# Four heads per pass on 128 partitions: block transposes on VectorE, block-diagonal fp32 bounds, score operands built by DMA, and an FFN in chunks of 512 tokens

## The chip, the cores and the metric

The kernel runs on one core of one Trainium2 chip. The metric is the device time of one execution in microseconds. A core has these engines: TensorE (PE in the profile; its weight loads are the row PEld), VectorE (DVE), ScalarE (ACT), GpSimd (POOL) and SyncE (SP, which here only issues DMA).

## The reference

An attention that looks only at the best chunks of keys, followed by a gated feed-forward network (FFN). Batch 4, 8 heads, 768 positions, 64 dimensions a head; the FFN sees 3072 tokens of 512 and has 1536 hidden channels.

```python
k_min, k_max = min and max of k over chunks of 32 positions      # 24 chunks
ub = sum_d max(q*k_min, q*k_max)                                 # upper bound per query and chunk
top = the 6 best chunks by ub among the causal ones              # per query
scores = (q @ k.T) / 8, masked to the chosen chunks and to the past
attn = softmax(scores) @ v                                       # heads side by side -> x, 512 wide
xn = x / sqrt(mean(x*x) + 1e-6) * rms_g
out = (silu(xn @ w_gate) * (xn @ w_val)) @ w_out
```

## The kernel before

It takes two heads at a time (16 pairs). It loads q and k with positions on partitions, transposes them on TensorE in fp32 and spreads the result on ScalarE and VectorE. The bounds use sum(relu(q)\*k_max - relu(-q)\*k_min): both parts stand on 128 partitions, so that one fp32 matmul gives 128 queries' bounds for up to 24 chunks. A query's threshold is its sixth best bound. The choice is written as 24 more rows under q, against rows of 30000 under k, so that the score matmul itself drops chunks. The causal triangle is added by one more matmul.

```python
# prep of a pair, per group of 128-position blocks
nc.tensor.transpose(pq[...], qnat[...], ident_f[:])                     # L158, fp32, likewise pk L177
nc.scalar.activation(out=QM[0][0:D, cols], in_=pq[0:D, :], func=ACT.Relu)
# ... three more relus, copies to QS and KE on ScalarE and VectorE, min and max of pk over chunks
# selection, per 128 queries and head (12 units a pair)
nc.tensor.matmul(ubp[:, 0:n_i], QM[hl][:, i*P:(i+1)*P], KM[hl][:, 0:n_i], ...)   # L213, fp32
# VectorE adds the causal mask and takes the best eight, GpSimd compares with the threshold (L253)
nc.tensor.transpose(stp[0:n_i, :], selq[:, 0:n_i], ident_b[:])          # L224
nc.vector.tensor_copy(QS[hl][D:D+n_i, i*P:(i+1)*P], stp[0:n_i, :])
# scoring, per head, 256 queries and group kg of 256 keys
nc.tensor.matmul(sc[:, e, :], keh[:, kb*P:(kb+1)*P], qsh[:, qcols], ...)          # L279
nc.tensor.matmul(sc[:, e, e*P:(e+1)*P], ident_b[:], trimask[:], ...)    # L284, the last group only
nc.scalar.activation(out=pt[:], in_=sc[:], func=ACT.Exp, scale=SCALE)   # 128x512
nc.tensor.matmul(avn[:], pt[:, e, s*P:(s+1)*P], vext[:, kb, hl, :], ...)          # L303
emit_ffn_slice(1)                                     # one piece of the FFN, if there is one
# ... [cut] after a batch's four pairs: x statistics, transposes of x, and its FFN pieces are queued,
# in a chunk of 512 and one of 256 tokens: 12+4 and 12+2 pieces
```

The softmax here doesn't subtract the row's maximum and nothing guards it: scores larger than these inputs give would overflow.

Of the kernel before, what the change touches and what calls it, by code (L numbers as in the profile page):

```python
# [8 lines left out]
FP32 = mybir.dt.float32  # L9
# [5 lines left out]
BIGE = 30000.0  # L15
BIGT = -30000.0
BIGC = 1.0e30
THRFLOOR = -5.0e29
# [3 lines left out]
def kernel(  # L22
# [14 lines left out]
    assert (P, D) == (128, 64) and S % 256 == 0  # L37
    CH = 32
    NCH = S // CH
    NT = S // P  # L40
    NQT = S // 256
    NP = H // 2
    DM = H * D
    DFF = moe_w_gate.shape[1]
    NHT = DFF // P
    NTOK = B * S
    NTT = NTOK // P
# [4 lines left out]
    prep = ctx.enter_context(tc.tile_pool(name="prep", bufs=3))  # L52
    headp = ctx.enter_context(tc.tile_pool(name="headp", bufs=6))
    sel = ctx.enter_context(tc.tile_pool(name="sel", bufs=8))
    work = ctx.enter_context(tc.tile_pool(name="work", bufs=6))
    evict = ctx.enter_context(tc.tile_pool(name="evict", bufs=6))
    hhp = ctx.enter_context(tc.tile_pool(name="hhp", bufs=NHT + 4))
    ffn = ctx.enter_context(tc.tile_pool(name="ffn", bufs=3))
    psA = ctx.enter_context(tc.tile_pool(name="psA", bufs=6, space=bass.MemoryType.PSUM))
    psF = ctx.enter_context(tc.tile_pool(name="psF", bufs=2, space=bass.MemoryType.PSUM))  # L60

    ident_f = const.tile([P, P], FP32, name="ident_f")
    masks.make_identity(nc, ident_f[:])
    ident_b = const.tile([P, P], BF16, name="ident_b")
    nc.vector.tensor_copy(ident_b[:], ident_f[:])

    trimask = const.tile([P, P], BF16, name="trimask")
    nc.gpsimd.memset(trimask[:], 0.0)
    nc.gpsimd.affine_select(
        out=trimask[:], in_=trimask[:], compare_op=ALU.is_ge, fill=BIGT,  # L70
        base=0, pattern=[[1, P]], channel_multiplier=-1,
    )

    cmf = const.tile([P, NT, NCH], FP32, name="cmf")
    nc.gpsimd.memset(cmf[:], 0.0)
    for g4 in range(4):
        nc.gpsimd.affine_select(
            out=cmf[32 * g4:32 * (g4 + 1), :, :],
            in_=cmf[32 * g4:32 * (g4 + 1), :, :],
            compare_op=ALU.is_ge, fill=-BIGC,  # L80
            base=g4, pattern=[[4, NT], [-1, NCH]], channel_multiplier=0,
        )

    e_all = const.tile([NCH, S], BF16, name="e_all")
    nc.gpsimd.memset(e_all[:], BIGE)
    nc.gpsimd.affine_select(
        out=e_all[:], in_=e_all[:], compare_op=ALU.is_ge, fill=0.0,
        base=0, pattern=[[1, S]], channel_multiplier=-CH,
    )
    nc.gpsimd.affine_select(  # L90
        out=e_all[:], in_=e_all[:], compare_op=ALU.is_ge, fill=0.0,
        base=CH - 1, pattern=[[-1, S]], channel_multiplier=CH,
    )

    eps6 = const.tile([P, 1], FP32, name="eps6")
    nc.gpsimd.memset(eps6[:], 1.0e-6)
    thrfloor = const.tile([P, 1], FP32, name="thrfloor")
    nc.gpsimd.memset(thrfloor[:], THRFLOOR)

    rmsg = const.tile([P, NP], FP32, name="rmsg")  # L100
    nc.sync.dma_start(out=rmsg[:], in_=moe_rms_g.rearrange("(g p) -> p g", p=P))

    ss_all = const.tile([P, NTT], FP32, name="ss_all")
    ri_all = const.tile([P, NTT], FP32, name="ri_all")

    xnat = [persist.tile([P, DM], BF16, name=f"xnat{tt}") for tt in range(NTT)]
    xsT = persist.tile([P, NP, NTOK], BF16, name="xsT")

    sel_count = [0]
    ffn_queue: list = []  # L110

    def emit_ffn_slice(n=1):
        for _ in range(n):
            if ffn_queue:
                ffn_queue.pop(0)()

    def emit_prep(b, pr):
        h0 = 2 * pr
        qnat = prep.tile([P, NT, 2, D], FP32, name="qnat")
        knat = prep.tile([P, NT, 2, D], FP32, name="knat")  # L120
        vext = prep.tile([P, NT, 2, D + 1], BF16, name="vext")
        for hh in range(2):
            nc.sync.dma_start(
                out=qnat[:, :, hh, :],
                in_=q[b, h0 + hh, :, :].rearrange("(blk pp) d -> pp blk d", pp=P),
            )
        for hh in range(2):
            nc.scalar.dma_start(
                out=knat[:, :, hh, :],
                in_=k[b, h0 + hh, :, :].rearrange("(blk pp) d -> pp blk d", pp=P),  # L130
            )
        nc.gpsimd.memset(vext[:, :, :, D:D + 1], 1.0)
        for hh in range(2):
            nc.gpsimd.dma_start(
                out=vext[:, :, hh, 0:D],
                in_=v[b, h0 + hh, :, :].rearrange("(blk pp) d -> pp blk d", pp=P),
            )

        kmx = prep.tile([P, NCH], FP32, name="kmx")
        kmn = prep.tile([P, NCH], FP32, name="kmn")  # L140

        KE, QS, QM, KM = [], [], [], []
        for hl in range(2):
            ke = headp.tile([D + NCH, S], BF16, name="ke")
            qs = headp.tile([D + NCH, S], BF16, name="qs")
            qm = headp.tile([P, S], FP32, name="qm")
            km = headp.tile([P, NCH], FP32, name="km")
            nc.sync.dma_start(out=ke[D:D + NCH, :], in_=e_all[:])
            nc.gpsimd.memset(qs[D:D + NCH, :], 0.0)  # L149
            KE.append(ke)  # L150
            QS.append(qs)
            QM.append(qm)
            KM.append(km)

        for blk0, nb in ((0, 4), (4, 2)):
            pq = psF.tile([P, nb * P], FP32, name="pq", tag="bank")
            for j in range(nb):
                nc.tensor.transpose(  # L158
                    pq[:, j * P:(j + 1) * P],
                    qnat[:, blk0 + j, :, :].rearrange("p h d -> p (h d)"),  # L160
                    ident_f[:],
                )
            cols = slice(blk0 * P, (blk0 + nb) * P)
            nc.scalar.activation(out=QM[0][0:D, cols], in_=pq[0:D, :], func=ACT.Relu)
            nc.scalar.activation(out=QM[0][D:2 * D, cols], in_=pq[0:D, :],
                                 func=ACT.Relu, scale=-1.0)
            nc.scalar.activation(out=QM[1][0:D, cols], in_=pq[D:2 * D, :],
                                 func=ACT.Relu, scale=-1.0)
            nc.scalar.activation(out=QM[1][D:2 * D, cols], in_=pq[D:2 * D, :],
                                 func=ACT.Relu)  # L170
            nc.scalar.activation(out=QS[0][0:D, cols], in_=pq[0:D, :], func=ACT.Copy)
            nc.vector.tensor_copy(QS[1][0:D, cols], pq[D:2 * D, :])

        for blk0, nb in ((0, 4), (4, 2)):
            pk = psF.tile([P, nb * P], FP32, name="pk", tag="bank")
            for j in range(nb):
                nc.tensor.transpose(  # L177
                    pk[:, j * P:(j + 1) * P],
                    knat[:, blk0 + j, :, :].rearrange("p h d -> p (h d)"),
                    ident_f[:],  # L180
                )
            cols = slice(blk0 * P, (blk0 + nb) * P)
            c0 = blk0 * (P // CH)
            ncv = nb * (P // CH)
            nc.vector.tensor_reduce(
                out=kmx[:, c0:c0 + ncv],
                in_=pk.rearrange("p (c t) -> p c t", t=CH),
                axis=AXX, op=ALU.max,
            )
            nc.vector.tensor_reduce(  # L190
                out=kmn[:, c0:c0 + ncv],
                in_=pk.rearrange("p (c t) -> p c t", t=CH),
                axis=AXX, op=ALU.min, negate=True,
            )
            nc.scalar.activation(out=KE[0][0:D, cols], in_=pk[0:D, :], func=ACT.Copy)
            nc.vector.tensor_copy(KE[1][0:D, cols], pk[D:2 * D, :])  # L196

        nc.vector.tensor_copy(KM[0][0:D, :], kmx[0:D, :])
        nc.vector.tensor_copy(KM[0][D:2 * D, :], kmn[0:D, :])
        nc.vector.tensor_copy(KM[1][0:D, :], kmn[D:2 * D, :])  # L200
        nc.vector.tensor_copy(KM[1][D:2 * D, :], kmx[D:2 * D, :])
        return dict(vext=vext, KE=KE, QS=QS, QM=QM, KM=KM, h0=h0)

    def emit_selection(st):
        units = [(i, hl) for i in range(NT) for hl in range(2)]
        ubps = {}
        selqs = {}

        def emit_ub(u):
            i, hl = u  # L210
            n_i = min(NCH, 4 * i + 8)
            ubp = psA.tile([P, NCH], FP32, name="ubp", tag="bank")
            nc.tensor.matmul(  # L213
                ubp[:, 0:n_i], st["QM"][hl][:, i * P:(i + 1) * P],
                st["KM"][hl][:, 0:n_i], start=True, stop=True,
            )
            ubps[u] = ubp

        def emit_transpose(u):
            i, hl = u  # L220
            n_i = min(NCH, 4 * i + 8)
# [271 lines left out]
```

## Time and profile before

628.95 us, the median of three runs (625.08 to 629.42). The first fence is from the page of the kernel before. The first line is each engine's busy time, its share of the span and its instructions. In the other two the span is cut in 40 equal slices: the first shows TensorE's busy share in tenths, the second the clock it was granted in tenths of full speed.

```profile
PE 496.7 (79%) x3242; PEld 323.7 (52%) x3264; DVE 335.8 (54%) x1422; ACT 309.4 (49%) x613; POOL 213.6 (34%) x389
...
PE   2057878778996979878997988877897897969975
...
PEclk9999975665898997765798897776789796858999
```

TensorE looks like the bound at 79%, but its clock dips to 0.5 to 0.7 once in each batch. The windows view shows what these stretches are. Each row is one stretch in us: its length, busy time and instruction count of each engine, granted clock, DMA share and GB/s.

```profile
core 0: us, PE busy (x) PEld busy (x) DVE busy (x) ACT busy (x) POOL busy (x), PEclk, DMA share, GB/s
...
50.00:161.00 111.00, 90.47 (x605) 67.56 (x606) 72.18 (x348) 57.77 (x112) 31.36 (x71) 0.72 0.27 44
161.00:254.00 93.00, 81.42 (x545) 49.37 (x549) 47.90 (x186) 48.71 (x101) 36.04 (x58) 0.90 0.19 38
254.00:303.00 49.00, 40.21 (x270) 29.39 (x269) 34.42 (x168) 27.96 (x54) 14.92 (x34) 0.58 0.31 50
...
565.00:628.00 63.00, 51.17 (x276) 27.50 (x279) 17.22 (x31) 27.50 (x55) 21.82 (x24) 0.96 0.07 26
```

I read these cuts off the instructions: no FFN matmul runs in 50:161 and in 254:303, and there the clock is 0.72 and 0.58. From 161 to 254 the FFN of the first batch fills the attention of the second, and the clock is 0.90. The left-out rows repeat this: filled 303:396 and 445:542, not filled 396:445 and 542:565. A batch has 30 FFN pieces for 48 places to put one, so each batch runs out of them. In all, 232 us are attention without FFN, 283 us attention with it, 50 us start, 63 us FFN alone at the end.

Two of the groups of TensorE that the change replaces are these (from the page's groups: line, engine, operation, output and inputs, shapes and count, then busy time and mean ns of one, then idle time ahead of it and who ended it):

```profile
L213 PE MATMUL ubp<-km,qm 128*128 128x24 f32 (+4 forms) x384 | 84.7, 319 | 0.1
...
L158 PE MATMUL pq<-ident_f,qnat 128*128 128x128 f32 x96 | 23.2, 352 | 27.5 <-issue 16.0 <-DMA qnat<-in_q_dram 7.6 <-DVE m_237 L243 3.5
```

The program has 192 bounds, 12 a pair: the profile shows two instructions for each of these fp32 matmuls, hence x384. "A bound" with a price below is one such instruction. These spans overlap on TensorE, so a mean of 319 ns is not what one bound costs. That needs the distance from one start to the next.

### The profile page before, as it was taken

The page shows a single profiled execution, that of the slowest core. Times are in us where ns is not written, and L with a number is a line of the kernel's source. Part 1 is how long each engine was busy: PE and PEld are TensorE (multiplying, and loading weights), DVE is VectorE, ACT ScalarE, POOL GpSimd, SP SyncE. Part 2 cuts the span into 40 slices and gives each one's busy share as a digit, 9 for nine tenths or more (in the row PEclk, how much of TensorE's full clock was granted, in tenths as well). Part 3 has the DMA queues.
Part 4 walks back from the last instruction along what each step waited for, and adds up shares of the span by engine and source line. Part 5 has one row for each costly group of instructions (what it writes and reads, how often), then busy time and mean ns, then how long its engine had stood idle before and what let it go on. Part 6 is the DMA issues. An engine that isn't in the chain of part 4 may idle for free.

```text
span 627.6 us, 9983 instructions
## 1 busy us (share of the span) xinstructions
PE 496.7 (79%) x3242; PEld 323.7 (52%) x3264; DVE 335.8 (54%) x1422; ACT 309.4 (49%) x613; POOL 213.6 (34%) x389
## 2 busy tenths in 40 slices
PE   2057878778996979878997988877897897969975
PEld 1045666565554556565554465555554475544443
DVE  2066657577465365677474365577553465553321
ACT  3035273473747255473748156373748147157431
POOL 6052422422272162413282072413353051304432
PEclk9999975665898997765798897776789796858999
DMA  9994232322022131423021222412100100000010
GB/s 174 208 185 67 15 61 37 41 57 38 4 15 53 68 41 28 75 56 38 5 16 40 80 24 47 74 31 14 13 6 1 42 26 2 36 0 1 19 48 35
DMA packets 83060, 28.57 MB, mean 46 GB/s; under 512 B 76608, under 2 KB 78912, under 8 KB 83008
## 3 DMA queue, kind: packets, MB, share of 16 engines
q0 software_dynamic: 27696, 7.87, 11.9%
q1 hardware_dynamic: 30224, 13.77, 8.6%
q10 hardware_dynamic: 25088, 6.29, 4.7%
q8 instruction: 26, 0.43, 0.3%
q14 instruction: 26, 0.21, 0.1%
HBM read 28.31 MB, written 6.29 MB: 55 GB/s over the span
## 4 chain that ended last, share of the span: by engine, by line
PE 57%; ACT 17%; DVE 11%; DMA 5%; issue 5%; POOL 4%; SPq 0%; ACTq 0%; DVEq 0%; POOLq 0%
PE opsum L394 11%; PE gp L368 10%; PE ubp L213 8%; PE vp L373 7%; PE sc L279 6%; ACT pt L293 6%; DMA qnat<-in_q_dram 5%; PE stp L224 5%; PE avn L303 4%; POOL selq L253 3%; DVE tg L382 2%; PE pq L158 2%; PE pk L177 2%; ACT sg L378 2%; ACT vs L380 2%
## 5 line engine op out<-in xcount | busy, mean ns | idle before, releaser
L293 ACT ACTIVATE pt<-sc 128x512 bf16<-128x512 f32 x192 | 110.7, 594 | 124.1 <-PE sc L284 98.8
L386 POOL TENSOR_TENSOR hh<-tg,vs 128x512 bf16<-128x512 bf16 (+1 forms) x96 | 87.3, 910 | 189.4 <-ACT vs L380 89.0
L382 DVE SCALAR_TENSOR_TENSOR tg<-sg,gp 128x512 bf16<-128x512 bf16 (+1 forms) x96 | 53.1, 553 | 95.3 <-ACT sg L378 91.9
L279 PE MATMUL sc<-qs,ke 88*128 88x256 bf16 x384 | 100.9, 347 | 2.1 <-ACT pt L293 1.8
L378 ACT ACTIVATE sg<-gp 128x512 bf16<-128x512 f32 (+1 forms) x96 | 47.1, 490 | 109.9 <-PE gp L368 106.1
L303 PE MATMUL avn<-vext,pt 128*128 128x65 bf16 x768 | 70.7, 219 | 26.2 <-ACT pt L293 24.9
L368 PE MATMUL gp<-xsT,wg 128*128 128x256 bf16 (+1 forms) x372 | 81.8, 338 | 12.0 <-ACT vs L380 7.4
L213 PE MATMUL ubp<-km,qm 128*128 128x24 f32 (+4 forms) x384 | 84.7, 319 | 0.1
L303 PEld LDWEIGHTS <-pt 128*128 128x128 bf16 x768 | 53.0, 115 | 57.2 <-ACT pt L293 46.7
L373 PE MATMUL vp<-xsT,wv 128*128 128x512 bf16 (+1 forms) x382 | 81.1, 335 | 0.2
L213 PEld LDWEIGHTS ubp<-km,qm 128*128 128x128 f32 x384 | 71.8, 248 | 14.2 <-DVE qs L225 3.1
L149 POOL MEMSET qs<- 24x768 bf16 x32 | 23.6, 740 | 146.6 <-PE sc L284 100.3
L394 PE MATMUL opsum<-wo,hh 128*128 128x512 bf16 x280 | 68.5, 402 | 2.9 <-DVE ke L196 1.3
L224 PE MATMUL stp<-ident_b,selq 128*8 128x128 bf16 (+2 forms) x192 | 44.8, 255 | 30.1 <-POOL selq L253 23.4
L380 ACT ACTIVATE vs<-vp 128x512 bf16<-128x512 f32 (+1 forms) x96 | 47.1, 490 | 24.4 <-PE vp L373 13.3
L225 DVE COPY qs<-stp 8x128 bf16<-8x128 bf16 (+2 forms) x192 | 39.8, 215 | 32.6 <-PE stp L224 28.2
L368 PEld LDWEIGHTS <-wg 128*128 128x128 bf16 x384 | 38.2, 105 | 36.2 <-issue 18.6
L373 PEld LDWEIGHTS <-wv 128*128 128x128 bf16 x384 | 38.8, 101 | 27.8 <-issue 3.2
L284 PE MATMUL sc<-trimask,ident_b 128*128 128x128 bf16 x192 | 50.8, 272 | 0.0
L394 PEld LDWEIGHTS <-hh 128*128 128x128 bf16 x288 | 29.6, 103 | 39.8 <-issue 9.9
L279 PEld LDWEIGHTS <-ke 88*128 88x128 bf16 x384 | 40.7, 121 | 8.9
L158 PE MATMUL pq<-ident_f,qnat 128*128 128x128 f32 x96 | 23.2, 352 | 27.5 <-issue 16.0
(513 smaller groups left out, 638.6 us busy)
## 6 DMA issues: line engine op xcount, KB each, us to landing
knat<-in_k_dram ACTq DMA_DIRECT2D x32, 192.0 KB
qnat<-in_q_dram SPq DMA_DIRECT2D x32, 192.0 KB
out_dram<-osb SPq DMA_DIRECT2D x24, 256.0 KB
vext<-in_v_dram POOLq DMA_DIRECT2D x32, 96.0 KB, 3.3
wg<-in_moe_w_gate_dram POOLq DMA_DIRECT2D x1, 1536.0 KB, 14.7
wv<-in_moe_w_val_dram POOLq DMA_DIRECT2D x1, 1536.0 KB, 22.1
wo<-in_moe_w_out_dram POOLq DMA_DIRECT2D x1, 1536.0 KB, 32.1
ke<-e_all SPq DMA_DIRECT2D x32, 36.0 KB
```

The costliest lines, as they stand in the source:

```text
L213: nc.tensor.matmul(ubp[:, 0:n_i], st["QM"][hl][:, i * P:(i + 1) * P], st["KM"][hl][:, 0:n_i], start=True, stop=True,)
L224: nc.tensor.transpose(stp[0:n_i, :], selq[:, 0:n_i], ident_b[:])
L279: nc.tensor.matmul(sc[:, e, :], keh[:, kb * P:(kb + 1) * P], qsh[:, qcols], start=True, stop=(not last_group),)
L293: nc.scalar.activation(out=pt[:], in_=sc[:], func=ACT.Exp, scale=SCALE)
L303: nc.tensor.matmul(avn[:], pt[:, e, s * P:(s + 1) * P], vext[:, kb, hl, :], start=(kg == 0 and e == 0), stop=(last_group and e == 1),)
L368: nc.tensor.matmul(gp[:], wg[:, g, ht * P:(ht + 1) * P], xsT[:, g, cols], start=(g == 0), stop=(g == NP - 1),)
L373: nc.tensor.matmul(vp[:], wv[:, g, ht * P:(ht + 1) * P], xsT[:, g, cols], start=(g == 0), stop=(g == NP - 1),)
L378: nc.scalar.activation(out=sg[:], in_=gp[:], func=ACT.Tanh, scale=0.5)
L380: nc.scalar.activation(out=vs[:], in_=vp[:], func=ACT.Copy)
L382: nc.vector.scalar_tensor_tensor(out=tg[:], in0=sg[:], scalar=1.0, in1=gp[:], op0=ALU.add, op1=ALU.mult,)
L386: nc.gpsimd.tensor_tensor(out=hh[ht][:], in0=tg[:], in1=vs[:], op=ALU.mult)
L394: nc.tensor.matmul(ops[j][:], hh[ht][:, th * P:(th + 1) * P], wo[:, ht, :], start=(ht == 0), stop=(ht == NHT - 1),)
```

## The change

Its intent: use all 128 partitions with four heads in a pass (8 passes), take small hand-offs and fp32 work off TensorE, and let the FFN start sooner. Block transposes of 32x32 on VectorE put the four heads' dimensions on the four groups of 32 partitions, in two halves of the dimensions. The bounds become sum(q\*k_min + relu(q)\*(k_max-k_min)), as four fp32 matmuls that accumulate, with block-diagonal weights for four heads and 288 queries as columns. The first 192 positions have at most six chunks and skip the choice. GpSimd casts q and k to bf16, and DMA copies SBUF to SBUF gather each head's 64 rows and the 24 mask rows. Exps cover two heads, the triangle is a VectorE multiply after the exp, and the FFN runs in chunks of 512 tokens as soon as 512 are ready, two pieces per unit (a unit is four heads, 256 queries and up to 256 keys; there are 48).

The diff, cut to its core:

```diff
-        for hh in range(2):
-            nc.sync.dma_start(
-                out=qnat[:, :, hh, :],
-                in_=q[b, h0 + hh, :, :].rearrange("(blk pp) d -> pp blk d", pp=P),
-            )
+            for a in range(4):
+                nc.sync.dma_start(
+                    out=t[32 * a:32 * (a + 1)].rearrange("r m j h d -> r m (j h d)"),
+                    in_=src[b, 4 * g + a, :, :].rearrange("(m r j) d -> r m (j d)", r=32, j=4),
+                )
... [cut]
+                nc.vector.transpose(
+                    out=st[nm + "T"][:, dh, :].rearrange("p (m r j) -> p m j r", r=32, j=4),
+                    in_=st[nm + "raw"][:, :, :, dh, :],
+                )
+                hb = half.tile([P, 2, S], BF16, name="hb")
+                eng.tensor_copy(hb[:], st[nm + "T"][:])
+                for dh in range(2):
+                    for a in range(4):
+                        nc.sync.dma_start(
+                            out=dst[bi][32 * dh:32 * (dh + 1), a, :],
+                            in_=hb[32 * a:32 * (a + 1), dh, :],
+                        )
... [cut]
+                for t in range(4):
+                    if t < 2:
+                        rhs = st["qT"][:, t, Q0 + i * W:Q0 + (i + 1) * W]
+                    else:
+                        rhs = st["qR"][:, t - 2, i * W:(i + 1) * W]
+                    nc.tensor.matmul(ubp[:, 0:W], bd[:, t, :], rhs, start=(t == 0), stop=(t == 3))
... [cut]
+            nc.vector.transpose(out=mt[:], in_=mk[:].rearrange("p j c -> p (j c)"))
+            for a in range(4):
+                nc.sync.dma_start(
+                    out=QH[bi][D:KR, a, Q0:S], in_=mt[32 * a:32 * a + NCH, :],
+                )
... [cut]
-                    if last_group:
-                        nc.tensor.matmul(
-                            sc[:, e, e * P:(e + 1) * P], ident_b[:], trimask[:],
-                            start=False, stop=True,
-                        )
+        if last:
+            dg = pt[:].rearrange("p a (e w) -> p a e w", e=2)[:, :, :, 0:P]
+            nc.vector.tensor_tensor(
+                out=dg, in0=dg,
+                in1=tri[:].unsqueeze(1).unsqueeze(1).to_broadcast([P, 4, 2, P]),
+                op=ALU.mult,
+            )
... [cut]
+        if o + P == CW:
+            queue_ffn(c)
... [cut]
+    for piece in prep_pieces(0):
+        piece()
+    fold_g()
... [cut]
+    order = [(0, 0), (0, 1), (1, 0), (1, 1), (0, 2), (1, 2)]
```

Here `fold_g()` multiplies two weight matrices by the RMS gains on VectorE; in the kernel before the program has it after the first batch.

## The prediction

> **What bounds it now.** TensorE: busy 497 of 628 us (79%, busy table), 57% of the chain that ended last; VectorE 336 us, ScalarE 309, GpSimd 214. Three things hide in that 79%.
> 1. Attention alone is slow. First scores run at 50.6 us, the first FFN matmul near 160. In 60:160 (windows view) the granted clock is 0.69: fp32 transposes, 24-column fp32 bounds, mask transposes, mask-adding matmuls, and waits for small GpSimd and ScalarE steps. Where FFN fills in (165:183) the clock is 1.00 and TensorE 98% busy. The mean is 0.823, with low spells in each batch (slice row).
> 2. The start: q and k land beside 4.7 MB of weights (chain waits for q up to 36 us).
> 3. The tail: 256-column FFN chunks on two PSUM banks idle 0.53 us in every 1.57.
>
> **What changes, at full clock** (start-to-start distances in undisturbed stretches: 512-column matmul 0.215 us, fp32 transpose 0.21, bound 0.20, value matmul 0.055, score 0.11).
> - TensorE loses 192 fp32 transposes (41 us), 384 bounds (77), 192 mask transposes (20), 192 mask adds (11), 96 value matmuls (5); gains 64 fp32 bounds of 288 columns, estimated at 0.5 us (32). Kept: FFN 187, scores 38 (were 42), values 37, x transposes 6. From about 428 to 300 us.
> - ScalarE loses q splitting and k copies (about 107 us) and table reloads; exps go from 192x594 ns to 96 larger (estimated 88 us). Sum about 190.
> - VectorE gains 32 fp32 block transposes of 768 (the Trainium skill, "Vector Engine (DVE) Microarchitecture Reference", 3.8: one element per cycle per lane; 512-element PSUM copies take 0.69 us here, so I estimate 0.9 us), reductions, triangle multiplies; loses PSUM copies and small steps. Sum about 225.
> - GpSimd gains bf16 copies, relu and block diagonals, about 8 us per pass (estimate from the 0.73 us memset of 768); loses compares and memsets. Sum about 195.
> - DMA gains about 20 SBUF copies per pass, a pass ahead, hidden except in the first.
>
> **On the critical path.** TensorE still bounds; nearly all of its saving counts. FFN starts after 6 of 48 units rather than a whole batch. 11 units have no FFN (6 first, about 5 between first and second chunk), about 5 us each at low clock: 55 us. 37 filled units: 2.35 us of attention plus two FFN pieces of 1.9, 6.2 ideal, about 7 real: 260. Tail: about 22 pieces, 46 us. Start to first scores: 38-45. Output and stalls (single value accumulator, three FFN banks, late GpSimd): 20. Sum about **425 us**, ratio 0.68. The Trainium skill, "TensorE: Matmul & The Clock Gate", parts 1 and 4, says that the clock follows TensorE's activity and that transposes don't count alike; the trace agrees (0.69 against 1.00). So the clock should rise to 0.88-0.95.
>
> Range 385 to 475. Faster by over 2%: 0.97; within 2%: 0.015; slower: 0.015.
>
> **What would show it.** First scores at 35-45 us, first FFN at 60-80; mean clock above 0.87; TensorE busy 340-370 us (85%); ScalarE about 190, VectorE 225, GpSimd 195; steady stretches with TensorE over 90% busy and FFN lines leading the chain; a dense tail near 45 us at full clock; one or two dips in the slice row.
>
> **What would make it wrong.** VectorE and GpSimd getting in each other's way, so that bounds arrive late and TensorE waits in order; block transposes at several ns per element; SBUF copies queued behind loads; low clock staying in the gaps; fp32 bounds dearer than 0.5 us.

## The result, and the profile after

438.2 us, the median of four runs (435.0 to 440.99), beside 628.99 us for the kernel before (four runs of the same rounds). The ratio is 0.697 (95% interval 0.693 to 0.701): faster, and inside the range that was predicted. Every ratio here is the mean time of one kernel's fast runs over that of the other's of the same rounds, so it is not quite the ratio of the medians quoted. All outputs are right. The same lines of the page, now of the changed kernel:

```profile
PE 320.6 (74%) x2144; PEld 181.0 (42%) x2144; DVE 258.9 (60%) x544; ACT 178.7 (41%) x265; POOL 183.4 (42%) x229
...
PE   0230084099897994888769986889899998789996
...
PEclk9985575558999896799959998799999999989999
```

VectorE is now at 60% and TensorE at 74%; the clock is low until about 100 us (its first 22 us are not on record and counted as full) and dips briefly near 165 and 220 us. The stretches, again cut by where FFN matmuls run:

```profile
core 0: us, PE busy (x) PEld busy (x) DVE busy (x) ACT busy (x) POOL busy (x), PEclk, DMA share, GB/s
0.00:62.00 62.00, 12.34 (x30) 7.66 (x30) 34.02 (x70) 1.28 (x1) 24.72 (x46) 0.75 1.14 162
62.00:107.00 45.00, 26.28 (x209) 18.69 (x210) 31.30 (x65) 19.47 (x24) 11.62 (x18) 0.62 0.45 102
107.00:156.00 49.00, 43.41 (x308) 23.34 (x307) 30.50 (x58) 25.73 (x39) 30.41 (x34) 0.97 0.62 92
156.00:181.00 25.00, 17.93 (x166) 13.10 (x166) 21.27 (x54) 11.25 (x14) 9.83 (x14) 0.73 0.71 116
181.00:370.00 189.00, 165.72 (x1163) 93.21 (x1160) 118.70 (x265) 97.91 (x150) 83.44 (x95) 0.95 0.24 54
370.00:433.00 63.00, 54.91 (x275) 24.98 (x273) 23.13 (x38) 23.01 (x39) 23.37 (x23) 0.97 0.09 34
```

| part of the run | before, us | predicted, us | after, us |
|---|---|---|---|
| start until first scores | 50 | 38 to 45 | 62 |
| attention without FFN | 232 | 55 | 45+25 = 70 |
| attention with FFN | 283 | 260 | 49+189 = 238 |
| FFN alone, output, stalls | 63 | 46+20 | 63 |

So of the 195 us between the two profiled spans, 162 came out of the stretches in which attention runs with no FFN beside it, 45 out of the filled ones, and the start gave 12 back. The new groups (from the longest list of groups of the changed kernel):

```profile
L148 DVE STREAM_TRANSPOSE kT<-kraw 128x768 f32<-128x768 f32 x16 | 24.0, 1534 | 3.7 <-DMA kraw<-in_k_dram 3.7
...
L209 PE MATMUL ubp<-qT,BD_131 128*128 128x288 f32 x32 | 11.1, 469 | 29.9 <-DVE qT L148 29.9
...
L209 PE MATMUL ubp<-qraw,BD_130 128*128 128x288 f32 x32 | 9.7, 429 | 0.0
```

Now the start, from the timeline of the changed kernel (start, length, engine and line, operation, count, and in brackets the idle time ahead and who ended it):

```profile
40.35 2.21 DVE L392 TENSOR_SCALAR wv<-wv,rmsg 128x1536 bf16<-128x1536 bf16 x4 [5.15 <-DMA wv<-in_moe_w_val_dram]
...
47.05 0.47 DVE L212 STREAM_TRANSPOSE ubn<-ubp 128x288 f32<-128x288 f32 x1
...
50.58 1.46 POOL L157 CAST hb<-qT 128x1536 bf16<-128x1536 f32 x1
50.94 1.70 DVE L231 TENSOR_TENSOR mk<-ubn,m_239 128x576 bf16<-128x576 f32 x1
...
53.49 3.16 SPq L239 DMA_DIRECT2D QH_127<-mt  x4
...
62.04 0.33 PE L269 MATMUL sc<-QH_127,KH_124 88*128 88x256 bf16 x2 [0.52 <-DMA QH_127<-hb]
```

VectorE works in order. The gains' multiply waits for the second weight matrix until 40.35 us, and the transposes of the first pass's bounds, whose matmuls had been done by 25.1 us, stand behind it, and behind the second pass's k transposes and first maximum, until 47.05. The mask can then be copied only at 53.5. GpSimd in turn casts the first pass's q at 50.58, behind work of the second pass that needs VectorE, and its copies are issued from 57.31 on. The first scores come at 62.04, not at 38 to 45, and the first FFN matmul at 107.7, not at 60 to 80.

### The profile page after: what moved, and what is told of

Read it like the earlier page. It is cut to its first block, busy times and chain, and to the rows that moved or that the text cites. A ratio compares the mean times of both kernels' runs of the same rounds, so it can differ in the third digit from the quotient of the medians.

```text
span 433.3 us, 6106 instructions
## 1 busy us (share of the span) xinstructions
PE 320.6 (74%) x2144; PEld 181.0 (42%) x2144; DVE 258.9 (60%) x544; ACT 178.7 (41%) x265; POOL 183.4 (42%) x229
## 4 chain that ended last, share of the span: by engine, by line
PE 39%; DVE 27%; DMA 11%; issue 9%; POOL 8%; ACT 3%; SPq 3%; POOLq 0%; DVEq 0%; ACTq 0%
PE op L375 12%; PE gp L357 8%; PE vp L357 8%; DMA wv<-in_moe_w_val_dram 6%; DVE qT L148 4%; PE sc L269 4%; DVE tg L366 4%; PE ubp L209 4%; DVE xs L331 3%; PE avn L298 3%; DVE junk L323 3%; POOL ri_all L329 2%; DMA vext<-in_v_dram 2%; DVE kT L148 2%; DVE xnat L312 2%
## 5 line engine op out<-in xcount | busy, mean ns | idle before, releaser
L275 ACT ACTIVATE pt<-sc 128x768 bf16<-128x768 f32 (+1 forms) x96 | 84.3, 916 | 142.3 <-PE sc L269 140.6
L370 POOL TENSOR_TENSOR hh<-tg,vs 128x512 bf16<-128x512 bf16 x72 | 84.3, 1174 | 93.2 <-ACT vs L364 37.9
L357 PE MATMUL gp<-xsT,wg 128*128 128x512 bf16 x288 | 78.2, 392 | 3.7 <-DVE tg L366 2.1
L357 PE MATMUL vp<-xsT,wv 128*128 128x512 bf16 x288 | 76.7, 388 | 1.0 <-DVE tg L366 0.6
L366 DVE SCALAR_TENSOR_TENSOR tg<-th,gp 128x512 bf16<-128x512 bf16 x72 | 49.0, 681 | 46.3 <-ACT th L362 46.2
L375 PE MATMUL op<-wo,hh 128*128 128x512 bf16 x288 | 65.8, 383 | 0.0
L362 ACT ACTIVATE th<-gp 128x512 bf16<-128x512 f32 x72 | 43.3, 602 | 53.7 <-PE gp L357 53.6
L364 ACT ACTIVATE vs<-vp 128x512 bf16<-128x512 f32 x72 | 43.2, 600 | 21.4 <-PE vp L357 17.8
L298 PE MATMUL avn<-vext,pt 128*128 128x65 bf16 x672 | 38.6, 206 | 12.9 <-DVE xnat L312 6.2
L269 PE MATMUL sc<-QH_128,KH_125 88*128 88x256 bf16 (+1 forms) x144 | 22.4, 282 | 15.2 <-DMA QH_128<-hb 13.0
L269 PE MATMUL sc<-QH_127,KH_124 88*128 88x256 bf16 (+1 forms) x144 | 25.9, 319 | 3.8 <-DMA QH_127<-mt 2.5
L148 DVE STREAM_TRANSPOSE kT<-kraw 128x768 f32<-128x768 f32 x16 | 24.0, 1534 | 3.7 <-DMA kraw<-in_k_dram 3.7
```

The lines of the kernel that those rows point to most:

```text
L148: nc.vector.transpose(out=st[nm + "T"][:, dh, :].rearrange("p (m r j) -> p m j r", r=32, j=4), in_=st[nm + "raw"][:, :, :, dh, :],)
L269: nc.tensor.matmul(sc[:, hl, 256 * e:256 * e + qn], KH[bi][0:KR, a, kb * P:(kb + 1) * P], QH[bi][0:KR, a, qs:qs + qn], start=True, stop=True,)
L275: nc.scalar.activation(out=pt[:, 2 * hp:2 * hp + 2, 0:W], in_=sc[:, :, 0:W], func=ACT.Exp, scale=SCALE,)
L298: nc.tensor.matmul(avn[:, a, :], pts[kg][:, a, off:off + P], vext[:, kb, a, :], start=(kb == 0 and a == 0), stop=(kb == nkb - 1 and a == 3 ...
L357: nc.tensor.matmul(ps[:], w[:, g, ht * P:(ht + 1) * P], x[:, g, :], start=(g == 0), stop=(g == NP - 1),)
L362: nc.scalar.activation(out=th[:], in_=gp[:], func=ACT.Tanh, scale=0.5)
```

## The experiments

The edits are against the changed kernel unless another is named. A difference in us below is the difference of two ratios times 629. The runs were made on three chips, each beside the kernel before, whose median was 628.7 to 629.0 us.

| run | us | ratio to before |
|---|---|---|
| changed kernel | 438.2 | 0.697 |
| fold_late | 421.2 | 0.670 |
| hb2 | 429.4 | 0.684 |
| both | 414.1 | 0.659 |
| rows256 | 484.4 | 0.771 |
| rows256_actload | 469.9 | 0.747 |
| both_actload | 431.6 | 0.687 |
| both_dummy | 417.9 | 0.665 |
| before_bounds_x2 | 673.2 | 1.070 |
| after_bounds_x2 | 463.6 | 0.737 |
| mask_on_pe | 439.4 | 0.696 |
| ffn_per_batch | 436.7 | 0.693 |
| cw256 | 447.4 | 0.713 |

### fold_late: weight scaling after the second pass's mask

```diff
     def fold_g():
+        rmsg_late = ev.tile([P, NP], FP32, name="rmsg_late")
+        nc.vector.scalar_tensor_tensor(
+            out=rmsg_late[:], in0=quads[1]["mt"][:, 0:NP], scalar=0.0, in1=rmsg[:],
+            op0=ALU.mult, op1=ALU.add,
+        )
... [cut] rmsg_late in place of rmsg in the scaling
-    fold_g()
... [cut] in the loop over units:
+        if i == 3:
+            fold_g()
```

The edit does not only move the call: it adds a data dependence on the second pass's mask, so that the scaling cannot be placed before it. (That moving the call alone would leave VectorE's compiled order as it was is not shown: no run does that.)

> The changed kernel, with the scaling of the two weight matrices held back until the second pass has its mask (it reads a copy of the gains that depends on it). Theory A: the start is long because VectorE works in order and the scaling, waiting for the weights until 40.4 us, holds up the first pass's bound transposes. Then first scores come at 36 to 44 us instead of 62, and the time falls by 16 to 26 us (438 to about 415). Rival B: the start is bound by DMA (loads of two passes and the weights at about 190 GB/s), and moving the scaling changes first scores by less than 5 us and the time by less than 6.

Measured: 421.2 us, 17.5 us less, and first scores at 43.3 us. Theory A holds. From its timeline:

```profile
26.18 0.48 DVE L212 STREAM_TRANSPOSE ubn<-ubp 128x288 f32<-128x288 f32 x1
...
28.04 0.76 DVE L231 TENSOR_TENSOR mk<-ubn,m 128x576 bf16<-128x576 f32 x1
...
43.26 0.46 PE L270 MATMUL sc<-QH,KH 88*128 88x256 bf16 x2 [2.44 <-DMA QH<-hb]
```

The bound transpose runs at 26.18 instead of 49.09 us for the second half. The rest of the start is still there: the copies of q, not the masks, are now last.

### hb2: two buffers for the bf16 copy

```diff
-    half = ctx.enter_context(tc.tile_pool(name="half", bufs=1))
+    half = ctx.enter_context(tc.tile_pool(name="half", bufs=2))
... [cut] to find room: junk with bufs=1, xs with bufs=2
```

The reason lies in a second gap of the changed kernel, from its timeline:

```profile
79.10 0.29 POOL L178 TENSOR_TENSOR dk<-kmx,kmn 128x48 f32<-128x48 f32 x1 [13.64 <-DVE kmn L169]
...
80.43 1.47 POOL L157 CAST hb<-qT 128x1536 bf16<-128x1536 f32 x1
...
86.54 1.59 PE L269 MATMUL sc<-QH_128,KH_125 88*128 88x256 bf16 x6 [12.79 <-DMA QH_128<-hb]
```

TensorE waits 12.79 us for copies whose cast GpSimd starts only at 80.43, behind `dk` of the third pass, which had waited 13.64 us for VectorE.

> The changed kernel with two buffers instead of one for the bf16 copy that the SBUF copies read (two scratch buffers made smaller to find room). Theory A: the second gap (TensorE idle 12.8 us at 73 to 86 us) comes from GpSimd's order: the cast of the second pass's q stands behind the third pass's block diagonal, because of the single buffer. With two buffers that gap falls below 6 us and the time by 5 to 13 us; first scores stay near 60 us since the weight scaling still holds up VectorE. Rival B: the copies' own time (5 us of issue per eight) makes the gap; the time changes by less than 4 us.

Measured: 429.4 us, 8.5 us less, first scores still at 61.5. In its timeline the copies start at 67.01 and the wait is 3.16 us:

```profile
67.01 4.97 SPq L160 DMA_DIRECT2D QH<-hb  x8
...
74.22 0.48 PE L269 MATMUL sc<-QH,KH 88*128 88x256 bf16 x2 [3.16 <-DMA QH<-mt]
```

Theory A holds.

### both

The two edits together.

> Both edits. If the two waits are separate, the gains add: 25 to 36 us less than the changed kernel, about 405 us. If the second only hides behind the first, no more than the better of the two.

Measured: 414.1 us, 24.0 us less; the parts would add to 26.0. First scores come at 38.9 us, the first FFN at 83.4. It falls just short of the range that I gave, but the waits are almost separate. This version beats both kernels. It is the fastest one run, and its first scores come when I had predicted them; its first FFN is still later than the 60 to 80 us of the prediction.

### rows256: contiguous transposes, 256 B packets

```diff
-                    in_=src[b, 4 * g + a, :, :].rearrange("(m r j) d -> r m (j d)", r=32, j=4),
+                    in_=src[b, 4 * g + a, :, :].rearrange("(m r) d -> r m d", r=32),
... [cut] and out= with "r m j h d -> r (m j) (h d)"
-                    out=st[nm + "T"][:, dh, :].rearrange("p (m r j) -> p m j r", r=32, j=4),
+                    out=st[nm + "T"][:, dh, :].rearrange("p (m j r) -> p m j r", r=32, j=4),
```

> The changed kernel with loads that put token m*128+j*32+r on partition r, so that each DMA packet has 256 B instead of 1 KB, and the block transposes write contiguous rows. Result right. Theory A: the fp32 transposes take 1.53 us for 768 elements instead of my estimate of 0.9 because they write with a step of 16 B; contiguous they take 0.95 to 1.05 us, VectorE's busy time falls by about 17 us, and the time by 0 to 10 us, less what the smaller packets cost at the start (first scores 2 to 6 us later). Rival B: fp32 transposes run at half rate however they write: 1.5 us stays, and the time rises by 0 to 6 us.

Measured: 484.4 us, 46.6 us more. The groups of its transposes, against 1534 ns above:

```profile
L148 DVE STREAM_TRANSPOSE qT<-qraw 128x768 f32<-128x768 f32 x16 | 15.1, 961 | 14.5 <-POOL hb L157 14.4
L148 DVE STREAM_TRANSPOSE kT<-kraw 128x768 f32<-128x768 f32 x16 | 14.9, 951 | 4.2 <-DMA kraw<-in_k_dram 4.2
```

So theory A is right about the instruction: the step of 16 B in the write costs 0.58 us of 1.53. It is wrong about the time. SyncE's queue, in the changed kernel and then in this one (the length is from the start of the first issue to the end of the last, gaps included):

```profile
5.10 3.44 SPq L125 DMA_DIRECT2D kraw<-in_k_dram  x4
9.22 4.57 SPq L125 DMA_DIRECT2D qraw<-in_q_dram  x4
18.44 5.03 SPq L160 DMA_DIRECT2D KH_124<-hb  x8
```

```profile
9.78 19.92 SPq L125 DMA_DIRECT2D kraw<-in_k_dram  x4
29.75 16.03 SPq L125 DMA_DIRECT2D qraw<-in_q_dram  x4
45.89 8.18 SPq L160 DMA_DIRECT2D KH<-hb  x8
```

The eight loads of the second pass go out over 3.44+4.57 us with 1 KB packets and over 19.92+16.03 us with 256 B (one of these, at 17.64 us, is on record for 12.06 us alone), and the operand copies of the first pass, in the same queue, go out at 45.89 instead of 18.44. But the first scores come only 2 us later (64.2): the weights land earlier here (the second matrix's multiplies start at 35.37 us, not at 40.35), and the loads take over as what is waited for. The loss lies between the first FFN (108 us in both) and the last scores (418.6 against 367.5 us), where the compiled order of the instructions also differs from the changed kernel's.

### rows256_actload: the same, loads from ScalarE's queue

```diff
-                nc.sync.dma_start(
+                nc.scalar.dma_start(
                     out=t[32 * a:32 * (a + 1)].rearrange("r m j h d -> r (m j) (h d)"),
```

> The version with 256 B packets (484 us), its q and k loads issued from ScalarE's DMA queue instead of SyncE's, which keeps the SBUF copies and the output. Theory A: it was slow because loads with small packets take 4 to 12 us each of the one queue that also carries the operand copies; apart, the time comes back to 430 to 450 us. Rival B: it was slow because the small packets load the DMA engines, or because the compiled order of instructions is a worse one; the time stays above 460 us.

Measured: 469.9 us, 15.6 us less than rows256. By the number rival B stands: taking the loads out of SyncE's queue brings back a third of the loss, net of what it costs ScalarE. For the loads go out slowly from either engine. From ScalarE's timeline:

```profile
24.57 26.48 ACTq L125 DMA_DIRECT2D kraw<-in_k_dram  x4
...
61.89 0.81 ACT L275 ACTIVATE pt<-sc 128x768 bf16<-128x768 f32 x1
```

These four loads go out over 26.48 us; each is on record for only 0.3 us, and ScalarE does nothing else in the gaps. Four more follow until 60.6 us, and the first exp, behind them in ScalarE's order, comes at 61.89 although the first scores begin at 51.5. How much of the remaining 31 us is this, DMA load or the compiled order, stays open.

### both_actload: 1 KB loads from ScalarE's queue

The one-line edit of rows256_actload, on both.

> The version with both edits (414 us), q and k loads issued from ScalarE's DMA queue. Theory A: operand copies of the first passes still wait behind the second pass's loads in SyncE's queue; first scores come at 33 to 37 us instead of 38.9 and the time falls by 3 to 10 us. Rival B: with 1 KB packets the queue costs nothing more: within 3 us, or longer, where ScalarE's exps wait behind loads whose buffer is not free.

Measured: 431.6 us, 17.3 us more than both: rival B. First scores come at 43.2 us instead of 38.9, the first FFN at 96.3 instead of 83.4. With 1 KB packets, too, four loads go out over 20.67 us from 8.78 us and four over 9.29 us from 51.77 us, and the exp behind the latter starts at 61.10, just after the last of them ends (61.05). So ScalarE's work does wait behind loads, and small packets alone are not why loads from ScalarE are slow. The Trainium skill, "DMA: Bandwidth & Descriptors", section "Issuing engines are not separate DMA queues", says that issuing from several engines saves only the sequencer's time. This run agrees that nothing is gained, and shows that it can cost much (17.3 us) when the engine chosen has other work.

### before_bounds_x2: each bound of the kernel before twice

```diff
-            nc.tensor.matmul(
-                ubp[:, 0:n_i], st["QM"][hl][:, i * P:(i + 1) * P],
-                st["KM"][hl][:, 0:n_i], start=True, stop=True,
-            )
+            for _ in range(2):
+                nc.tensor.matmul( ... the same ... )
```

> The kernel before, with each fp32 bound matmul issued twice (the second overwrites the same result with the same values). Theory A (the prediction's): TensorE bounds, so what is added on it counts in full: 384 more instructions at 0.20 us and the lower clock make 70 to 100 us more. Rival B: before was bound by hand-offs between engines, and the extra matmuls fill waits: under 40 us more. In the stretch of attention alone the granted clock (0.69 before) should rise if it was low for lack of matmul activity.

Measured: 673.2 us, 44 us more, between the two ranges. A stretch at full clock of this run (bounds, then the next matmul) settles which:

```profile
189.18 1.71 PE L214 MATMUL ubp<-km,qm 128*128 128x8 f32 x14
190.74 0.59 PE L369 MATMUL gp<-xsT,wg 128*128 128x512 bf16 x2
```

From 189.18 to 190.74 is 1.56 us for 14, or 0.111 us each, not 0.20. 384 of these are 43 us at full clock, and 44 were measured. But not all run at full clock: 346 of the 768 bounds of this trace fall in half-clock time (96 of them before the clock's record begins), where one takes 0.213 us. So the added work is nearer to 60 us, and about three quarters of it counted (estimates). What is added on TensorE counts for the most part, as theory A says, but not in full, and its price at full clock was about half of what I had put in. The clock from 60 to 160 us is shown as 0.73 instead of 0.69; with the time that is not on record at half clock, it is about 0.59 against 0.57, so it hardly rose.

### after_bounds_x2: each bound of the changed kernel twice

The loop over the four bound matmuls stands twice; the second pass overwrites with the same values.

> The changed kernel with each of its fp32 bound matmuls issued twice. Theory A: TensorE bounds it too: 31 us busy more, and 25 to 35 us longer. Rival B: now that TensorE has slack and VectorE stands in the chain (27%), under 15 us longer.

Measured: 463.6 us, 24.7 us more for 64 more matmuls, shown as 128 instructions of 0.24 us (31 us). Just short of theory A's 25 to 35 us: about four fifths of TensorE's time still counts after the change.

### mask_on_pe: the triangle back on TensorE

```diff
-                        start=True, stop=True,
+                        start=True, stop=not last,
                     )
+                    if last:
+                        nc.tensor.matmul(
+                            sc[:, hl, 256 * e:256 * e + P], ident[:], tri[:],
+                            start=False, stop=True,
+                        )
... [cut] tri holds 0 and -30000, the VectorE multiply is gone
```

> The changed kernel with the old way of causal masking: TensorE adds a triangle of -30000 to the scores (192 matmuls of 128 columns, about 11 us at full clock), VectorE's triangle multiply (19 us) is gone. Theory A (TensorE bounds): 6 to 14 us longer. Rival B (VectorE and the hand-off from exp over the triangle to the value matmuls bound): 0 to 12 us shorter.

Measured: 439.4 us, 0.6 us less by the ratio, within the noise. VectorE is busy 239.9 us instead of 258.9, TensorE 326.2 instead of 320.6. That is the lower edge of rival B's range. As far as these runs can tell (the intervals of the two ratios are some 2.5 us each way), the two costs cancel: this part of the change gained nothing that shows.

### ffn_per_batch: FFN only after a whole batch

```diff
         if o + P == CW:
-            queue_ffn(c)
+            pending.append(c)
+        if tt % NT == NT - 1:
+            while pending:
+                queue_ffn(pending.pop(0))
... [cut] xtp bufs=3, hhp bufs=NHT + 2, junk bufs=1
```

> The changed kernel with the FFN work released only when a whole batch's attention is done, as the kernel before had it (one more x buffer; hidden buffers 16 to 14, one scratch buffer fewer). Theory A (the gain is mostly less TensorE work in attention): 8 to 25 us longer, from about 5 more units without FFN and a tail of about 32 pieces instead of 22. Rival B (the gain is mostly the earlier and better spread FFN): 60 us longer or more.

Measured: 436.7 us, 2.5 us less, about the width of the interval. Both theories are wrong: an FFN that can start after six units instead of a batch is worth nothing that shows here. Its windows show why:

```profile
core 0: us, PE busy (x) PEld busy (x) DVE busy (x) ACT busy (x) POOL busy (x), PEclk, DMA share, GB/s
63.00:126.00 63.00, 29.72 (x306) 21.25 (x308) 41.59 (x95) 23.80 (x29) 23.10 (x34) 0.72 0.59 94
126.00:351.00 225.00, 195.04 (x1401) 114.31 (x1424) 148.84 (x331) 121.76 (x183) 102.13 (x120) 0.94 0.35 67
351.00:435.00 84.00, 76.40 (x378) 35.18 (x382) 29.12 (x48) 31.58 (x54) 30.84 (x30) 0.98 0.10 38
```

Attention alone is now one stretch of 63 us instead of two of 45 and 25, and the tail is 84 us instead of 63. The amount of FFN is fixed: what is done early is missing later. This run also gives a like comparison, as its first batch's attention is all alone: 63 us, against 111 us (50:161) before. TensorE is busy 29.7 us of these 63, and was busy 90.5 of the 111; VectorE, with 41.6 us, is now the busier. Some of the work has moved into the longer start, though: from the beginning to the first FFN it is 126.5 us against 161.4.

### both_dummy: matmuls that nobody reads, where there is no FFN

```diff
             if ffn_queue:
                 ffn_queue.pop(0)()
+            elif warm is not None:
+                ps = psF.tile([P, 512], FP32, name="warm", tag="bank")
+                for a in range(4):
+                    nc.tensor.matmul(ps[:, 0:384], ident[:], warm[:, a, 0:384], start=True, stop=True)
```

> The version with both edits, with four matmuls of 384 columns on data of the unit, whose result nobody reads, once in each unit in which there is no FFN piece to fill in. Theory A (the prediction's: low clock in the units without FFN costs time, and it is low for lack of streaming work): the granted clock between first scores and first FFN rises from 0.66 to over 0.80, and the time falls by 2 to 10 us. Rival B: these stretches are bound by other engines, so the clock costs nothing there, and the added matmuls (about 0.7 us each time at full clock) lengthen it by 0 to 10 us.

Measured: 417.9 us, 3.8 us more than both. The stretch from first scores to first FFN, in both and in this run:

```profile
39.00:83.00 44.00, 22.27 (x190) 15.42 (x189) 30.68 (x60) 16.79 (x21) 9.31 (x15) 0.65 0.93 163
```

```profile
39.00:87.00 48.00, 32.45 (x244) 22.15 (x243) 34.87 (x76) 17.94 (x22) 10.49 (x15) 0.73 0.87 150
```

TensorE's busy time went from 22 to 32 us, the clock from 0.65 to 0.73, and the stretch got longer: rival B. VectorE is busy 31 of 44 us there and is closer to a bound than TensorE. But the clock stayed below the 0.80 that theory A asked for, so what a full clock would be worth there is not tested.

### cw256: FFN chunks of 256 tokens

```diff
-    CW = 512
+    CW = 256
... [cut] xtp bufs=4, and fill(2) for fill(1)
```

> The changed kernel with FFN chunks of 256 tokens (and twice as many pieces per filling). Theory A (512 matters): ScalarE and VectorE gain about 12 us each from the fixed part of their instructions (384 against 598/2 ns, 420 against 686/2), TensorE pays twice the weight loads: 4 to 20 us longer. Rival B: the finer pieces fill better and hide that: within 4 us, or shorter.

Measured: 447.4 us, 9.8 us more: theory A. ScalarE is busy 198 us instead of 179, weight loads 243 instead of 181. So chunks of 512 beat chunks of 256 by this much here. The kernel before ran 512 of every 768 tokens in chunks of 512 already, so about a third of it is the change's own gain (estimate).

## Why the prediction was right

**The sum was right** (425 predicted, 438 measured, a range of 385 to 475), and so was its main step: TensorE's time counts for the most part, before (44 us for some 60 added) and after (25 for 31). But three terms were mis-sized, and they partly cancelled: that the sum came within 13 us is in part luck.

1. **"Start until first scores: 38-45."** It measured 62. I had not asked in which order VectorE and GpSimd would take the work: the weight scaling holds VectorE until the weights land, and the single cast buffer turns GpSimd's order round. fold_late and hb2 show both, and both has first scores at 38.9. This is the largest miss: 17.5 us and 8.5 us alone, 24 us together.
2. **"Bound 0.20" and "fp32 transpose 0.21 us" at full clock.** These were distances at half clock; before 84 us, where the profile shows full clock without a record, one finds just these. From the kernel before, the bounds of a stretch at the recorded half clock (10 until the next start, 2.14 us) and of one at full clock (6 in 0.67 us):

```profile
89.16 2.29 PE L213 MATMUL ubp<-km,qm 128*128 128x8 f32 x10
91.30 0.38 PE L303 MATMUL avn<-vext,pt 128*128 128x65 bf16 x4
```

```profile
171.38 0.82 PE L213 MATMUL ubp<-km,qm 128*128 128x8 f32 x6
172.05 1.02 PE L368 MATMUL gp<-xsT,wg 128*128 128x512 bf16 x4
```

   That is 0.214 and 0.112 us. In the same way six fp32 transposes at 193.85 us took 0.72 us to the next start, 0.12 each. So the 384 bounds and 192 transposes are about 43+23 us at full clock, not 77+41, and TensorE lost about 75 us of full-clock work, not 128 (estimates from these distances). Even at half clock 75 us would be 150 of the 191 us gained; the rest has to be shorter waits, or kept work at a higher clock. The value matmul's 0.055 us was a half-clock distance as well: four at 190.75 us took 0.12 us to the next start, 0.03 each, so the work that was kept is over-priced too. The Trainium skill, "TensorE: Matmul & The Clock Gate", section "LDWEIGHTS (loading the stationary operand)", gives a formula by which a load of 128 columns takes 128/1.2 = 107 ns (an estimate from it). A bound with 8 columns is close to that at full clock (112 ns), so the page would have been nearer than my 0.20; that the load is what sets the distance is argued from the match alone, and at half clock the bound takes 214 ns, which the formula does not tell apart.
3. **VectorE "about 225".** It measured 259. The transposes are 1.53 us and not 0.9, which is 20 us over 32; rows256 shows that it is the step in the write. Some VectorE instructions also take longer beside GpSimd: the comparison for the mask took 1.70 us at 50.94 us, while GpSimd's cast ran from 50.58 to 52.04, and 0.76 us in fold_late, with no GpSimd instruction beside it. The Trainium skill, "SBUF — State Buffer", section "Who interferes with whom", says that a VectorE instruction with two SBUF inputs and a GpSimd instruction that reads SBUF exclude each other; this pair agrees. So does a case where VectorE began first (fold_late, 46.20 us): the comparison took 0.76 us, and the cast beside it 2.04 instead of 1.46 us.

The other figures held: ScalarE 179 us (predicted 190), GpSimd 183 (195), tail 63 (46+20). The mean clock is 0.881 in the profiled run and 0.874 to 0.881 in all four, at the lower edge of 0.88 to 0.95; with the first 22 us at half clock it is about 0.85 (estimate). TensorE's busy time, 321 us, is below the 340 to 370 given, and in the long filled stretch it is busy 88% (165.7 of 189), not over 90%. In the stretches without FFN "TensorE still bounds" does not hold by busy time: VectorE is busy 31.3 and 21.3 us of the 45 and 25, TensorE 26.3 and 17.9.

**Where the gain came from.** 162 of 195 us came out of attention without FFN, for two reasons that the prediction saw but did not weigh. One batch's attention alone fell from 111 us to 63 (ffn_per_batch). And less of it is alone: 232 us were about 2.1 batches' worth before, 70 are 1.1 now, since before, four batches have 192 places for some 120 pieces, and now 96 pieces go two to a unit over 48 units. The first effect, 48 us in one batch, is measured; taken 2.1 times it is about 100 us, which leaves out that the start, once in a run, took 12 us more. That the second makes up the rest is argued from the windows, and no run filled the kernel before more evenly. "FFN starts after 6 of 48 units" was given as a step of the gain, and ffn_per_batch shows that it was none. The triangle on VectorE was no gain either (mask_on_pe).

**The clock.** That it would rise was right (0.823 to 0.881; about 0.76 to 0.85 if the time that is not on record is taken at half clock, as the distances there say). The reason given, that transposes do not count, is shown by no run: in 62:107 of the changed kernel TensorE transposes no q or k, only 16 blocks of x (2.2 us), and the clock is still 0.62, beside about 0.56 before (estimate; the windows view's 0.72 counts 34 us without a record as full, and the prediction's 0.69 for 60:160 counts 24). Added matmuls moved it little and did not shorten the stretch (both_dummy).

**What stays open:** how the 46.6 us of rows256 divide among SyncE's queue, DMA load and compiled order; how the two reasons for the shorter time without FFN divide exactly; and which of the replaced steps (fp32 transposes and bounds on TensorE, the splitting of q on ScalarE, the small hand-offs) brought one batch's attention from 111 to 63 us. Only the triangle, the early FFN and the chunk size were taken back one at a time.

## What to carry to other kernels

Ask of an instruction that waits for a late DMA which other work stands behind it on its engine: here an 8-instruction weight scaling and one missing buffer were worth 24 us, while the triangle on VectorE and the early FFN, both intended, gained nothing that shows. Take start-to-start distances only together with the granted clock of that stretch, and check that this clock is on record: time without a record is counted as full speed. A filler such as an FFN is a fixed amount: releasing it earlier gained nothing here (that spreading it evenly helps is argued above, not shown).

## What the Trainium skill lacked or had wrong

- "DMA: Bandwidth & Descriptors", "Issuing engines are not separate DMA queues": it calls the issuing time usually small. Here four loads of 192 KB went out over 3.44 us with 1 KB packets and 19.92 us with 256 B (SyncE), over 26.48 us with 256 B and up to 20.67 us with 1 KB from ScalarE, and moving loads to a working ScalarE cost 17.3 us. What the engine waits for is not shown.
- "Vector Engine (DVE) Microarchitecture Reference", 3.8: one element per cycle per lane for a transpose. That section does not speak of how the result is written. An fp32 transpose of 768 took 0.95 to 0.96 us with contiguous writes and 1.53 us with writes 16 B apart.
- "TensorE: Matmul & The Clock Gate", parts 1 and 4: activity sets the clock, and transposes do not count as busy alike. The profile's busy time does not foretell it: in 86:101 of the changed kernel, mostly score and value matmuls (12 of the 107 instructions are transposes of x), TensorE was busy 13.71 of 15 us at a granted clock of 0.50, and in 181:370 busy 88% at 0.95. What is counted stays unclear.
